# Two attention + feed-forward layers on one core: VectorE's exp in five passes instead of six, its steps and the side work paced by VectorE's queue, and the last 1024 queries of the first layer in chunks of 256

## The chip, the core and the metric

The kernel runs on one core of one Trainium2 chip. A core has five engines that run their own instruction streams and wait for one another through semaphores: TensorE (PE, matrix products; its weight loads are shown as PEld), VectorE (DVE), ScalarE (ACT, the engine with exp and tanh), GpSimd (POOL) and SyncE (SP, here the issuer of DMAs). The metric is the device time of one execution in microseconds (us); lower is better.

## The reference

Input x is 2048 tokens of 512 values, in bf16. The same weights are used twice:

```python
def _A_ref(x, wqkv, wo):                 # 32 heads of 16
    qkv = (x @ wqkv).reshape(B, S, 3, H, Dh).transpose(2, 0, 3, 1, 4)
    q, k, v = qkv[0], qkv[1], qkv[2]
    p = softmax(einsum("bhqd,bhkd->bhqk", q, k) * Dh ** -0.5)
    o = einsum("bhqk,bhkd->bhqd", p, v)
    return o.transpose(0, 2, 1, 3).reshape(B, S, D) @ wo

def _B_ref(x, w1, w2):                   # 512 -> 1792 -> 512
    return einsum("bsf,fd->bsd", silu(einsum("bsd,df->bsf", x, w1)), w2)

x = A_x
x = x + _A_ref(layernorm(x), A_wqkv, A_wo)
x = x + _B_ref(layernorm(x), B_w1, B_w2)
x = x + _A_ref(layernorm(x), A_wqkv, A_wo)
x = x + _B_ref(layernorm(x), B_w1, B_w2)
```

The exps are the bulk: 2 layers x 32 heads x 2048 x 2048 of them, against matrix products with an inner dimension of 16 for the scores.

## The kernel before

**Tiling.** Heads go in blocks of four (hb, eight of them), each head padded to 32 rows, so that four heads fill the 128 rows of PE. Queries go in chunks: three of 512 and two of 256 in both layers (CHUNKS, L163). A *block* is one chunk of one head block (class Block, L683). A *unit* is the scores of one head for 512 columns: 128 keys x 512 queries in a chunk of 512, two key tiles x 256 queries in a chunk of 256. Its scores are K (stationary) times Q (moving), into PSUM; then exp; then p (moving) times V with a column of ones (vaug, stationary), which accumulates both output and row sum in PSUM.

**Two streams of exp.** The function stream (L712) emits everything between the first and the last exp. Units are taken in *groups* of three and two in turn (new_group). A group's scores lie in one PSUM tile s_ps, and ACT makes p_sb of it in one instruction, 128x1536 or 128x1024 (L997). The tile p_sb of three units has two buffers, that of two units one (L213). Beside a group, one more unit can go to DVE (extra, chosen by spare, L749): its scores go into one of the three PSUM banks of the pool g, and exp_on_dve (L755) makes exp by bits: scale to an integer (PSUM to SBUF), split off mantissa and exponent by two bitwise instructions, two steps of a polynomial, and a last step that multiplies by the exponent and writes the bf16 tile pd_sb. These six instructions are a *chain*. spare gives a new unit only when the chain is empty, a count of DVE's outstanding work (V.behind) is below PITCH, and a bank is free. One step of the chain is emitted after each group; the product with V comes DEFER = 4 groups after the unit was taken, that is three after its last step.

**Side work.** Everything else is cut into *pieces* (class Piece) in four lanes: ends (a block's division by the row sum, finish), keys (keys of the next layer for the first six head blocks), main (output projection, layer norm, feed-forward of a finished chunk, then what the next layer needs of it) and side (queries of the next chunk, other keys, V). After each group, pieces are stepped while a credit lasts, at most 1024 columns of matmul; the credit grows by pace(g), the work to do in this phase over the groups left in it. Matmuls without use (keep_busy, fillers) are put in where the sum of PE's work over three groups is below BUSY. PE's instructions stay in the order in which they are emitted (pin, L192); DVE's and ACT's order follow from it.

**The layer boundary.** Layer 2 can't start before layer 1's last chunk has gone through its feed-forward. So the first six head blocks of layer 2's first chunk start *early*, on the first 1536 keys alone (EK, NE at L161; part "early"), and get the other 512 keys later (part "late"), with a factor that joins the two. The head blocks 6 and 7 ("full") need all keys. If a block's queries are not made when its scores are emitted, need (L817) steps pieces until they are, however many.

**Order of stages.** Layer 1: chunks 0, 1, 2 (512 queries), 3, 4 (256). Layer 2: early blocks, full and late blocks of chunk 0, chunks 1, 2, then 3 and 4 (256). Ahead of the first exp lie the loads, the layer norm of x and the first keys, V and queries; after the last exp the tail, that is projection, layer norm and feed-forward of the last 256 queries and the store. DVE's instructions are all issued by one helper, so their line is L36; the products on PE are L193, its transposes L197.

## Time and profile before

| what | us |
|---|---|
| median of 3 runs | 1985.38 (1978.69 to 1989.32) |
| the profiled execution, its own time | 1986.21 |
| its span, first to last instruction | 1984.4 |
| first exp of L997 starts at | 53.0 |
| last stage ends, tail begins | 1952.0 |
| ACT busy / exps of L997 alone | 1837.1 / 1773.4 |
| DVE busy / its exp passes (e_sb, pd_sb) | 1467.3 / 972.2 |
| PE busy | 1659.2 |
| mean granted clock of TensorE | 0.953 |

The exps are 765 of 128x1536 and 765 of 128x1024; the six DVE passes belong to 271 units. Busy time of ACT is a union: an exp starts while the one before it drains, so 1773.4 us is less than the sum of the durations. PE's busy time is modelled from the starts of pipelined matmuls and says little on how near PE is to its limit. The granted clock is that of TensorE alone; the profile shows it at half speed in some stretches, most of them in the second layer. The kernel's stages have different lengths, so the 40 equal slices of the page mix them; a table by stage is read in the prediction.

### The profile page before, as it was taken

The page shows a single profiled execution, that of the slowest core. Times are in us where ns is not written, and L with a number is a line of the kernel's source. Part 1 is how long each engine was busy: PE and PEld are TensorE (multiplying, and loading weights), DVE is VectorE, ACT ScalarE, POOL GpSimd, SP SyncE. Part 2 cuts the span into 40 slices and gives each one's busy share as a digit, 9 for nine tenths or more (in the row PEclk, how much of TensorE's full clock was granted, in tenths as well). Part 3 has the DMA queues.
Part 4 walks back from the last instruction along what each step waited for, and adds up shares of the span by engine and source line. Part 5 has one row for each costly group of instructions (what it writes and reads, how often), then busy time and mean ns, then how long its engine had stood idle before and what let it go on. Part 6 is the DMA issues. An engine that isn't in the chain of part 4 may idle for free.

```text
span 1984.4 us, 31764 instructions
## 1 busy us (share of the span) xinstructions
PE 1659.2 (84%) x12915; PEld 558.3 (28%) x12915; DVE 1467.3 (74%) x2966; ACT 1837.1 (93%) x1690; POOL 13.0 (1%) x17
## 2 busy tenths in 40 slices
PE   4888888888888888898888888888888788888887
PEld 2222222222222223333322222222222222233333
DVE  6798877777867787678866687776777777756764
ACT  5799999999999999999999798999999999889994
POOL 2000000000000000000000000000000000000000
PEclk9999999999999999999999889997999999879998
DMA  4000000000000000000000000000000000000000
GB/s 159 1 1 1 1 1 1 1 1 1 1 1 1 1 1 1 1 1 2 1 1 1 1 1 1 1 1 0 7 6 1 1 1 11 1 1 3 11 1 12
DMA packets 8403, 11.99 MB, mean 6 GB/s; under 512 B 320, under 2 KB 7232, under 8 KB 8256
## 3 DMA queue, kind: packets, MB, share of 16 engines
q1 hardware_dynamic: 8256, 9.96, 1.5%
q8 instruction: 101, 1.65, 0.3%
q14 instruction: 46, 0.38, 0.1%
HBM read 7.86 MB, written 2.10 MB: 5 GB/s over the span
## 4 chain that ended last, share of the span: by engine, by line
ACT 58%; PE 22%; DVE 15%; issue 5%; ACTq 0%; DVEq 0%
ACT p_sb L997 55%; PE g L193 14%; PE s_ps L193 7%; DVE e_sb L36 6%; ACT t_sb L601 2%; DVE qa L36 1%; DVE pd_sb L36 1%; DVE KT L36 1%; PE g L197 1%; DVE st L36 1%; DVE amaxp L36 1%; DVE oT L36 1%; DVE sel L36 1%; DVE x_sb L36 1%; ACT p_sb L1097 0%
## 5 line engine op out<-in xcount | busy, mean ns | idle before, releaser
L997 ACT ACTIVATE p_sb<-s_ps 128x1536 bf16<-128x1536 f32 (+1 forms) x1530 | 1773.4, 1283 | 94.2 <-PE g L193 67.7
L193 PE MATMUL s_ps<-QT,KT 32*128 32x512 bf16 (+1 forms) x4788 | 621.3, 348 | 231.7 <-ACT p_sb L997 213.1
L193 PE MATMUL g<-p_sb,vaug 128*32 128x512 bf16 (+1 forms) x4788 | 515.8, 355 | 1.8 <-ACT p_sb L997 0.6
L193 PEld LDWEIGHTS <-KT 32*128 32x128 bf16 x5120 | 229.9, 92 | 778.5 <-issue 749.7
L36 DVE SCALAR_TENSOR_TENSOR e_sb<-e_sb 128x512 f32<-128x512 f32 x542 | 370.4, 683 | 5.3
L36 DVE TENSOR_SCALAR e_sb<-g 128x512 int32<-128x512 f32 x271 | 186.6, 688 | 195.0 <-PE g L193 190.3
L36 DVE TENSOR_SCALAR e_sb<-e_sb 128x512 int32<-128x512 int32 x542 | 229.4, 423 | 13.6
L36 DVE SCALAR_TENSOR_TENSOR pd_sb<-e_sb 128x512 bf16<-128x512 f32 x271 | 185.8, 686 | 28.1 <-PE g L193 18.4
L193 PEld LDWEIGHTS <-vaug 128*32 128x32 bf16 x5120 | 145.4, 96 | 203.0 <-issue 187.3
L193 PE MATMUL g<-w_sb,hT 128*128 128x512 bf16 x448 | 139.4, 385 | 1.7 <-DVE KT L36 0.5
L36 DVE SCALAR_TENSOR_TENSOR hT<-t_sb,g 128x512 bf16<-128x512 f32 x105 | 72.0, 686 | 82.4 <-ACT t_sb L601 80.9
L193 PE MATMUL g<-xnT,w_sb 128*128 128x512 bf16 x336 | 116.7, 415 | 0.6 <-DVE xnT L36 0.5
L193 PE MATMUL g<-QT,KT 32*128 32x512 bf16 (+1 forms) x332 | 107.3, 353 | 2.8 <-DVE QT L36 0.8
L193 PE MATMUL g<-pd_sb,vaug 128*32 128x512 bf16 (+1 forms) x332 | 107.9, 355 | 0.0
L193 PE MATMUL g<-xnT,wq_pad 128*128 128x512 bf16 x280 | 95.6, 397 | 0.5 <-DVE QT L36 0.5
L193 PE MATMUL g<-xnT,wk_pad 128*128 128x512 bf16 x256 | 85.7, 404 | 5.6 <-DVE e_sb L36 1.6
L601 ACT ACTIVATE t_sb<-g 128x512 f32<-128x512 f32 x105 | 71.1, 677 | 1.7 <-PE g L193 1.7
L36 DVE CAST qa<-g 128x512 bf16<-128x512 f32 x70 | 48.0, 686 | 29.8 <-PE g L193 29.5
L36 DVE TENSOR_SCALAR QT<-g,shiftcol 128x512 bf16<-128x512 f32 x70 | 52.3, 747 | 19.1 <-PE g L193 18.2
L36 DVE CAST oT<-g 128x512 bf16<-128x512 f32 (+1 forms) x86 | 50.3, 585 | 19.3 <-PE g L193 18.8
L193 PEld LDWEIGHTS <-w_sb 128*128 128x128 bf16 x560 | 41.5, 100 | 80.0 <-issue 76.6
L36 DVE TENSOR_SCALAR KT<-g,onescol 128x512 bf16<-128x512 f32 x60 | 44.8, 747 | 16.4 <-PE g L193 16.2
(82 smaller groups left out, 810.5 us busy)
## 6 DMA issues: line engine op xcount, KB each, us to landing
w_sb<-in_B_w_dram SPq DMA_DIRECT2D x2, 1792.0 KB, 13.6
x_sb<-in_A_x_dram SPq DMA_DIRECT2D x4, 512.0 KB, 5.6
out_dram<-x_sb SPq DMA_DIRECT2D x8, 256.0 KB, 2.1
wqk_raw<-in_A_wqkv_dram SPq DMA_DIRECT2D x4, 256.0 KB, 7.2
wv_sb<-in_A_wqkv_dram SPq DMA_DIRECT2D x1, 512.0 KB, 8.5
wo_sb<-in_A_wo_dram SPq DMA_DIRECT2D x1, 512.0 KB, 8.7
```

Of the source, the lines that this page charges most:

```text
L36: return op(*args, **kw)
L193: ins = nc.tensor.matmul(*args, **kw)
L197: ins = nc.tensor.transpose(*args)
L601: nc.scalar.activation(t_sb[:, 0 : n * w], box["h"], ACT.Tanh, scale=0.5)
L997: nc.scalar.activation(p_sb[:, 0:n, :].rearrange("p a b -> p (a b)"), s_ps[:, 0:n, :].rearrange("p a b -> p (a b)"), ACT.Exp, bias=float(B ...
```

## The change

Four things are changed; the rest of the diff passes names through (L.chunks for CHUNKS, L.nch for NCH).

1. **exp_on_dve.** Five instructions instead of six: the exponent is no longer split off. M is the mantissa with a constant exponent (4 << 23), read as an integer; a cubic in M is made in two steps, and the last one adds it to the scaled integer. The result is an int32 whose upper half word is the bf16 of the exp; the product with V reads these halves at a step of two, so there is no tile pd_sb. The constants and the bias of ACT's exp change with it.

```diff
-            e = epool.tile([P, 3, 512], FP32, name="e_sb", tag="e")
+            bits = epool.tile([P, 512], I32, name="bits", tag="bits")
+            M = epool.tile([P, 512], I32, name="M", tag="M")
...
             def split():
                 V.tensor_scalar(
-                    out=w, in0=bits, scalar1=0x007FFFFF, scalar2=0x3F800000,
+                    out=M[:], in0=bits[:], scalar1=0x007FFFFF, scalar2=4 << 23,
                     op0=ALU.bitwise_and, op1=ALU.bitwise_or, share=0.5,
                 )
-                V.tensor_scalar(
-                    out=bits, in0=bits, scalar1=0x7F800000, scalar2=None, op0=ALU.bitwise_and,
-                    share=0.5,
-                )
...
+            def square():
+                box["u"] = epool.tile([P, 512], FP32, name="u", tag="u", bufs=2)
+                V.scalar_tensor_tensor(
+                    out=box["u"][:], in0=M[:], scalar=float(A1), in1=M[:], op0=ALU.add, op1=ALU.mult
+                )
+            def cube():
+                V.scalar_tensor_tensor(
+                    out=box["u"][:], in0=box["u"][:], scalar=float(A0), in1=M[:],
+                    op0=ALU.add, op1=ALU.mult,
+                )
             def last():
-                p = ppool.tile([P, 512], BF16, name="pd_sb", tag="pd", bufs=1)
+                u = box["u"][:].bitcast(I32)
                 V.scalar_tensor_tensor(
-                    out=p[:], in0=u, scalar=float(C0), in1=bits.bitcast(FP32),
-                    op0=ALU.add, op1=ALU.mult,
+                    out=u, in0=box["u"][:], scalar=float(CURVE), in1=bits[:],
+                    op0=ALU.mult, op1=ALU.add,
                 )
+                return u.bitcast(BF16).rearrange("p (n h) -> p n h", h=2)[:, :, 1]
```

2. **When the chain's steps and its product are emitted.** Instead of one step a group, steps are emitted while DVE's counted queue is under 1000 ns, with at most two units between their third step and their product. The product comes from two groups after the last step on, ahead of the products of the same block. spare may take the extra unit from the next block when the one at hand is nearly done; DEFER, now only a limit there, goes from 4 to 6.

```diff
-            if chain:
+            V.pass_time(1331 if n == GU else 905)
+            while chain and V.behind < 1000:
+                if len(chain) == 3 and n_begun - n_made >= 2:
+
+                    break
+                n_begun += len(chain) == 3
                 p = chain.pop(0)()
                 if not chain:
-                    later[chain_of[0] + DEFER] = [(p[:], extra[chain_of[0]])]
-            V.pass_time(1331 if n == GU else 905)
+                    late.append((g + 2, p, extra[chain_of[0]]))
```

```diff
-            todo += later.pop(g, [])
             todo += [(p_sb[:, i, :], u) for i, u in enumerate(grp)]
+            for x in [x for x in late if x[0] <= g]:
+
+                b = x[2][0]
+                at = next((i for i, (_, u) in enumerate(todo) if u[0] is b), None)
+                if at is not None:
+                    todo.insert(max(at, kept), x[1:])
+                    late.remove(x)
```

3. **Chunks by layer.** Layer 1 has two chunks of 512 and four of 256, layer 2 keeps three and two.

```diff
-    CHUNKS = [(512 * i, 512) for i in range(NKC - 1)] + [(S - 512, 256), (S - 256, 256)]
-    NCH = len(CHUNKS)
+    def query_chunks(n):
+
+        whole = [(512 * i, 512) for i in range(NKC - n)]
+        return whole + [(at, 256) for at in range(S - 512 * n, S, 256)]
...
-    L1 = make_layer(1, 0)
+    L1 = make_layer(1, 0, 2)
...
-    L1.nxt = L2 = make_layer(2, NE)
+    L1.nxt = L2 = make_layer(2, NE, 1)
```

4. **Pace and order of the side work.** pace counts what the feed-forward of the chunks of a phase will bring (chain_cost) instead of a constant 55000; layer 1's last chunk and layer 2's early blocks are one phase ("end") in which the early stage no longer asks for the largest credit; AHEAD goes from 28 to 20. After an even group up to 1536 columns of pieces are stepped, after an odd one 1024. main goes ahead of keys while the next two blocks have their queries, and a query piece is held back while eight QT tiles are in use (q_live). To make room in SBUF, the tail's tanh tile and the sums of the first three early blocks lie in tiles of attn.

```diff
+        def order():
+
+            near = all(b.QT in b.L.QT for b in waiting[:2])
+            return (ends, main, keys, side) if near else (ends, keys, main, side)
...
+        def chain_cost(L, c):
+
+            w = L.chunks[c][1]
+            per_tile = 6 * 512 + FT * 512 + (5 * 512 if L.nxt is not None else 0)
+            return w // P * per_tile + FT * CT * w
...
-            if ph[1] == -1:
-                return 3072
-            if ph[1] < NKC - 1:
-                todo += max(len(here) - 1, 0) * 2560
-            elif any(b.c == NCH - 2 for b in here):
-                todo += 55000
+            full = [b for b in here if b.part != "early"]
+            to_end = ph[1] == "end"
+            for L, c in {(b.L, b.c) for b in full}:
+                if to_end or c != max(b.c for b in full):
+                    todo += chain_cost(L, c)
...
-            while (credit[0] > 0 or hurry or sum(busy) < BUSY) and ran < 1024:
+            while (credit[0] > 0 or hurry or sum(busy) < BUSY) and ran < most:
...
-                    t_sb = epool.tile([P, 3 * 512], FP32, name="t_sb", tag="e")
+                    t_sb = achunk_pool.tile([P, 4, D], BF16, name="t_sb", tag="attn")
+                    t_sb = t_sb[:].rearrange("p a b -> p (a b)").bitcast(FP32)
```

## The prediction, made before the changed kernel was run

> **What bounds the kernel now.** I read the page first (engine totals, chain), then cut the span into its stages, then the groups by shape, the waits, and one timeline. The page says that ScalarE (ACT) carries the span:

> ```profile
> span 1984.4 us, 31764 instructions
> PE 1659.2 (84%) x12915; PEld 558.3 (28%) x12915; DVE 1467.3 (74%) x2966; ACT 1837.1 (93%) x1690; POOL 13.0 (1%) x17
> ACT 58%; PE 22%; DVE 15%; issue 5%; ACTq 0%; DVEq 0%
> ```

> To see where ACT's missing 7% lies I cut at the first exp of each stage, found by counting the exps of L997 in issue order. Columns: stretch, length, busy time (and count) of PE, PEld, DVE, ACT, POOL, then TensorE's granted clock.

> ```profile
> 287.00:514.10 227.10, 192.63 (x1298) 59.66 (x1298) 176.44 (x352) 223.81 (x205) 0.00 (x0) 0.98 0.00 1
> 740.80:859.70 118.90, 103.60 (x1209) 42.31 (x1209) 83.73 (x179) 117.53 (x112) 0.00 (x0) 1.00 0.01 1
> 978.90:1130.00 151.10, 129.59 (x867) 41.39 (x867) 102.51 (x228) 132.77 (x125) 0.00 (x0) 0.93 0.00 1
> 1130.00:1243.60 113.60, 95.37 (x619) 27.46 (x618) 84.98 (x171) 98.17 (x90) 0.00 (x0) 0.86 0.00 1
> 1708.30:1838.90 130.60, 114.41 (x1181) 43.58 (x1179) 80.70 (x171) 117.90 (x111) 0.00 (x0) 0.84 0.01 3
> 1952.00:1984.40 32.40, 20.73 (x115) 11.32 (x114) 14.02 (x34) 3.71 (x5) 0.00 (x0) 0.79 0.03 9
> ```

> The rows are layer 1's chunk 1 (512 wide) and chunk 3 (256 wide), layer 2's early blocks, the rest of its chunk 0, its chunk 3, and the tail. Length minus ACT busy is idle: 3.3, 1.4, 18.3, 15.4 and 12.7 us. Over all eleven stages (53.0 to 1952.0, 1899 us) it is 93 us. So ACT is the limit in the steady stages; idle time gathers at the layer boundary and where the clock fell. Two stages of one shape, 740.8 (clock 1.00, idle 1.4) and 1708.3 (0.84, 12.7), price the clock: 0.16 below full over 130.6 us cost 11.3 us.

> The boundary's largest single idle is seen in the timeline:

> ```profile
> 1120.56 0.74 DVE L36 TENSOR_SCALAR hT<-x_sb,mvb,lny 128x512 bf16<-128x512 bf16 x2
> ...
> 1122.32 1.87 PE L193 MATMUL g<-xnT,wk_pad 128*128 128x512 bf16 x4 [0.52 <-DVE xnT L36]
> ...
> 1127.26 0.75 DVE L36 TENSOR_SCALAR QT<-g,shiftcol 128x512 bf16<-128x512 f32 x1 [0.48 <-PE g L193]
> ...
> 1128.07 0.39 PE L193 MATMUL s_ps<-QT,KT 32*128 32x512 bf16 x3 [0.84 <-DVE QT L36]
> ```

> The next block's queries were not there, so layer norm, transposes, the last key piece and the query piece of head block 6 ran one after another with the scores queued behind them on PE. ACT stood still for 8.1 us, then 1.3 and 1.7 more at half clock.

> ```profile
> ACT p_sb L997 <- PE g L193: 67.7, 92, 3.5
> ACT p_sb L997 <- PE s_ps L193: 23.5, 28, 8.1
> ```

> The 8.1 is the longest of the second row. The first row, exps waiting for the product with V, is the usual wait: the 1024-wide p_sb has one buffer (L213), so its next exp needs the product's matmuls done.

> **The change, part by part.** *Units moved to DVE.* A unit is the exp of 128 keys x 512 queries of one head; two layers of 32 heads x 16 x 4 make 4096. In issue order DVE did 271 and now does 320; ACT keeps 3776 of 3825. The exps' 1773.4 us (page, first group) over 3825 units is 0.464 us a unit; 49 fewer make **-22.7 us**, all on ACT, which sets the end.

> ```profile
> L36 DVE SCALAR_TENSOR_TENSOR e_sb<-e_sb 128x512 f32<-128x512 f32 x542 | 370.4, 683 | 5.3
> L36 DVE TENSOR_SCALAR e_sb<-e_sb 128x512 int32<-128x512 int32 x542 | 229.4, 423 | 13.6
> L36 DVE TENSOR_SCALAR e_sb<-g 128x512 int32<-128x512 f32 x271 | 186.6, 688 | 195.0 <-PE g L193 190.3
> L36 DVE SCALAR_TENSOR_TENSOR pd_sb<-e_sb 128x512 bf16<-128x512 f32 x271 | 185.8, 686 | 28.1 <-PE g L193 18.4
> ```

> (The answer by shapes: mean ns, then idle before.) A unit was 0.688 + 2 x 0.423 + 2 x 0.683 + 0.686 = 3.586 us; now 0.688 + 0.423 + 3 x 0.683 = 3.160. DVE's exp goes from 271 x 3.586 = 972 to 320 x 3.160 = 1011 us, +39, beside ACT. In the stage at 287 us DVE was 176 of 227 us busy; 44 units for 36 add 139.0 - 129.1 = 9.9, so 186 of about 222, 84%: no bound by sum. The three passes now read int32 through the two-input form, which has no row here; bounds 423 (int32, one input) and 747 (QT's row), nearest 683, taken. At 747 DVE gains 61 us of work, 3% of the span, hidden by ACT.

> *The boundary.* The feed-forward of layer 1's chunks now runs earlier: as the early blocks begin, lane main holds pieces of 82,944 columns, before 117,760 (nearly two chunks of 256 instead of one, 40,000 each, and what follows them). In the new issue order the last transpose of its keys stands 26 exps ahead of block 6's first scores, and that block's queries are 15 exps ahead; before, both fell in one burst of eleven pieces. I take off the 8.1, 1.3 and 1.7 and add 1 for what is spread out: **-10**. Bounds: 0 (idle moves ahead) and -30 (both boundary stages fall to the 1.5% idle of the stage at 287: 33.7 - 0.015 x 265 = 29.7).

> *PE.* 512 more matmul pairs of 256 columns: the 256-wide stage at 740.8 idled 1.4 us, the 512-wide one 3.3 per twice the time, so 0. Pieces per pair of exps in the early stage rise from 1583 to 1730 columns, 14 matmuls of 512 in all; 41 fillers come too, issued where PE has room. One such matmul is 0.229 us:

> ```profile
> 39.78 2.75 PE L193 MATMUL g<-wv_sb,xnT 128*128 128x512 bf16 x12
> ```

> 14 x 0.229 = 3.2, and groups with three pieces instead of two come in bursts: **+3**, between 0 and +9 (fillers on the path too).

> *Reading every second half word.* PE reads DVE's probabilities as bf16 at a step of two. No row here has a moving operand with a step. Bounds: 0, and half rate, 320 x 0.229 = 73 us of PE. The half-clock stage says how much PE time reaches ACT: 0.16 x 130.6 = 20.9 us of PE lost, 11.3 us idle, 54%; so +39. I take **0**, as the pattern still advances one column per read.
> [...]

> *Pacing.* A unit's product with V now comes two exps after its last pass (three before), and passes go out only while DVE's queue counts under 1.0 us. So the last is done 1.0 + 0.69 = 1.7 us later against 2 exps, 1773.4 / 765 = 2.3 us: 0.6 us of margin. Behind it on PE are the two products that free the 1024-wide p_sb. **+2** for some late ones; bounds 0 and the third rival's 48. Layer norm and evictions of one more chunk are some 8 us of DVE (16 more each of oT 0.416, rec 0.198 and attn 0.284 for 8 fewer of 0.684, 0.247 and 0.415: 3.6; the rest small layer-norm steps at 0.16), hidden under ACT in the 256-wide stages, where DVE was 70% to 86% busy. The tail's tanh tile and three of the early sums move into tiles of attn; the instructions there keep the waits that they had, so 0. Head (53.0) and tail (32.4) stay. No DMA is added or moved; SP's and POOL's queues are as before.

> Sum: -22.7 - 10 + 3 + 2 = -27.7. The profiled execution took 1986.2 us (1.8 around its span), 0.8 above the median of the three runs; 1986.2 - 27.7 = **1958.5**.

> **Rivals.** *Idle moves* (0.15): the burst goes, but the early stage, at 1730 columns a pair, pays it back; 1986.2 - 22.7 + 5 = 1968. For: its idle was already 18.3 us; against: the chunk at 740.8 carries 1536 columns a pair and idles 1.4.
> *Half-rate reads* (0.08): 1958.5 + 39 = 1997. For: no row; against: the columns are no more than before.
> *Late DVE units* (0.13): the slower side. At the margin of 0.6 us, any wait of DVE on PE between the last passes decides; its waits ahead of e_sb<-g are 190.3 us over 158. Each such wait makes the unit 1.7 + 1.2 - 2.3 = 0.6 us late; if a quarter of that reaches ACT at every unit, 320 x 0.15 = 48: 2006. It beats the gain from 0.09 us per unit (27.7 / 320). Against: ahead of the 332 products from pd_sb the trace of before shows 0.0 us of idle, with DVE 83% busy in the first stage.

> **How the numbers follow.** The forecast has 0.64. I count 0.5%, 10 us, as what a measurement can tell: bounds 1975 and 1995. Faster: 0.62 of the forecast's, 0.12 of the first rival's, 0.02 of half-rate reads with a smaller share = 0.76. Slower: 0.11 late units, 0.04 half-rate = 0.15. Same: 0.09. Range: low 1932 (the boundary's -30 with neither PE's 3 nor pacing's 2 paid is 1986.2 - 22.7 - 30 = 1933.5); high 1990, into the case of late units, which leaves 0.08 of the 0.13 and some of the half-rate reads outside. That the clock alone can move a stage by 11 us is why the range is wide on both sides.

> **What would show it.** x755 of each exp shape; u passes near 683 ns; no 8 us wait of ACT on scores at the boundary, whose two stages should idle under 25 us together; matmuls g<-u,vaug as long as g<-p_sb,vaug (400 ns), with no idle waiting for DVE u. Waits of PE on u, or of exps on PE g well over 67.7 us, make it wrong, as would a lower granted clock.

## The result, and the profile after

| | median, us | range of 12 runs | profiled execution | its span |
|---|---|---|---|---|
| before | 1979.0 | 1971.2 to 1989.5 | 1986.2 | 1984.4 |
| after | 1995.6 | 1990.2 to 2004.0 | 1991.5 | 1989.7 |

(The kernel before was measured anew, beside the changed one on one chip.) The ratio of the times is 1.0083, 95% interval 1.0057 to 1.0109: the changed kernel is 0.8% slower, where 1958.5 us, 1.4% faster than the execution it was reckoned from, was forecast. The two profiled executions lie 7 us above and 4 us below their medians, so their traces differ by 5 us only; what was gained and what was lost can be read in them all the same. (The rest goes with TensorE's granted clock: the profiled execution of the changed kernel has the highest of its twelve, 0.950, the others down to 0.939; more on this in the last section.) The page of the changed kernel (span, busy time of the engines, the chain's shares by engine):

```profile
span 1989.7 us, 33776 instructions
PE 1601.6 (80%) x13838; PEld 585.6 (29%) x14036; DVE 1537.5 (77%) x2990; ACT 1818.5 (91%) x1671; POOL 13.0 (1%) x17
ACT 55%; PE 22%; DVE 15%; issue 7%; ACTq 0%; DVEq 0%
```

ACT has 18.6 us less to do, as it should, and its idle time has grown by more: 1989.7 - 1818.5 = 171.2 us against 147.3. (PE has 198 matmul records fewer than weight loads, so its busy time is not compared.) The answer by shapes shows the units and their cost, and which exps wait:

```profile
L1045 ACT ACTIVATE p_sb<-s_ps 128x1536 bf16<-128x1536 f32 x755 | 1123.0, 1487 | 20.7 <-PE s_ps L198 16.0 <-PE g L198 3.9
L1045 ACT ACTIVATE p_sb<-s_ps 128x1024 bf16<-128x1024 f32 x755 | 797.3, 1056 | 100.9 <-PE g L198 95.7 <-ACT t_sb L613 0.3
L36 DVE TENSOR_SCALAR bits<-g 128x512 int32<-128x512 f32 x320 | 220.7, 690 | 159.6 <-PE g L198 149.3
L36 DVE SCALAR_TENSOR_TENSOR u<-M 128x512 f32<-128x512 int32 x320 | 220.6, 689 | 13.9 <-PE g L198 5.3 <-PE g L202 0.5
L36 DVE SCALAR_TENSOR_TENSOR u<-u,bits 128x512 int32<-128x512 f32 x320 | 219.8, 687 | 6.6
L198 PE MATMUL g<-p_sb,vaug 128*32 128x512 bf16 x2358 | 306.1, 398 | 0.0
L198 PE MATMUL g<-u,vaug 128*32 128x512 bf16 x202 | 75.7, 407 | 7.9 <-DVE u L36 5.1 <-DVE oT L36 1.0 <-DVE bits L36 0.7
```

The five passes and the strided product cost what was assumed. The idle time is on the odd exps, 128x1024, and ends when PE has done a product (g). The waits say the same (sum, count, longest):

```profile
ACT p_sb L1045 <- PE g L198: 99.5, 134, 3.4
ACT p_sb L1045 <- PE s_ps L198: 16.0, 27, 3.8
```

Against the kernel before, 32 us more in 42 more waits on products; the 8.1 us wait on scores at the boundary is gone. By stage (columns as in the prediction's first table):

```profile
289.10:517.40 228.30, 185.67 (x1285) 59.22 (x1305) 188.06 (x353) 220.20 (x202) 0.00 (x0) 0.97 0.00 1
517.40:648.70 131.30, 104.80 (x1173) 42.70 (x1188) 92.45 (x184) 117.29 (x110) 0.00 (x0) 0.88 0.00 1
648.70:767.70 119.00, 99.28 (x1182) 44.33 (x1197) 92.04 (x198) 110.49 (x99) 0.00 (x0) 0.94 0.01 2
887.10:1015.30 128.20, 107.39 (x1212) 46.28 (x1226) 97.12 (x215) 114.12 (x104) 0.00 (x0) 0.89 0.01 1
1015.30:1153.50 138.20, 118.25 (x813) 37.15 (x825) 112.49 (x228) 128.35 (x117) 0.00 (x0) 0.98 0.00 1
1153.50:1262.40 108.90, 91.75 (x625) 27.52 (x634) 75.52 (x149) 100.22 (x93) 0.00 (x0) 0.97 0.00 1
```

These are layer 1's chunk 1, three of its four chunks of 256 (the *quarters*: 517.4, 648.7 and 887.1), and the two boundary stages. The boundary's idle is 9.9 + 8.7 = 18.5 us (33.7 before): a gain of 15. The quarters idle 14.0, 8.5 and 14.1 us (the fourth 5.3), where the chunk 2 of 512 and the two old chunks of 256 that they replace idled 3.4, 1.4 and 9.1. Chunk 1 has 8.1 for 3.3. All stages together: 118.8 against 93.1.

What such an idle spot looks like, in the timeline of the first quarter (start, length, engine, line, operation, shapes, count, and in brackets the idle time before and what ended it):

```profile
597.82 1.02 ACT L1045 ACTIVATE p_sb<-s_ps 128x1024 bf16<-128x1024 f32 x1
...
599.22 1.46 ACT L1045 ACTIVATE p_sb<-s_ps 128x1536 bf16<-128x1536 f32 x1
...
601.07 0.29 PE L198 MATMUL g<-p_sb,vaug 128*32 128x256 bf16 x2
601.18 2.36 ACT L1045 ACTIVATE p_sb<-s_ps 128x1536 bf16<-128x1536 f32 x2
...
603.59 0.29 PE L198 MATMUL s_ps<-QT,KT 32*128 32x256 bf16 x2 [2.12 <-ACT p_sb L1045]
...
603.93 0.39 PE L198 MATMUL g<-p_sb,vaug 128*32 128x256 bf16 x4
...
604.07 0.49 PE L198 MATMUL g<-p_sb,vaug 128*32 128x256 bf16 x6
...
604.70 1.02 ACT L1045 ACTIVATE p_sb<-s_ps 128x1024 bf16<-128x1024 f32 x1 [1.16 <-PE g L198]
```

The row at 601.18 joins two exps under the shape of the first: one of 1536, then one of 1024. So ACT ran 1024, 1536, **1536, 1024**, 1024: the exp at 601.18 was issued ahead of the odd one that was emitted before it. PE stood still for 2.12 us, since its next scores need the PSUM tile of the exp that came last; then the products and the next odd exp, which needs the one 1024-wide p_sb back, ran in series, and ACT idled 1.16 us. ACT's issue order, in which the kernel is built, shows it without any time:

```
L1045 Activation p_sb<-s_ps 128x1024
L613 Activation t_sb<-g 128x512
L1045 Activation p_sb<-s_ps 128x1536
L613 Activation t_sb<-g 128x512
L1045 Activation p_sb<-s_ps 128x1536
L1045 Activation p_sb<-s_ps 128x1024 x2
```

There are 17 such *turns* in the changed kernel, ten of them in the quarters, and 5 in the kernel before, three of them in the two boundary stages; the traces show the same counts. Each stands where one block gives way to the next, and where this line of the loop holds the products of the new block back (the same line in both kernels):

```python
if odd and kept <= GU and unit[0].out is None and min(Lane.banks + o_free) > g:
    break
```

It breaks when no bank of the pool g is free, by the loop's own book, for the new block's output. The book returns a bank later when DVE's counted queue is long (`late` in Lane.step). The products that would free the 1024-wide p_sb then come behind the next scores, the odd exp isn't ready in its turn, and the scheduler issues the even one first. I call this a *hold*. Counted in both traces alike, ACT idles 36.5 us before the five exps from each turn on in the changed kernel and 11.3 us in the kernel before; 22.3 of the 36.5 lie in the quarters. All its other idle time, from the first exp on, is 109.6 against 110.6 us, although the boundary gave 15 of it back. So the theory was: holds, by the exps out of turn that they cause; and a smaller loss somewhere that eats the boundary's gain.

### The profile page after: what moved, and what is told of

It reads as the page before. It is cut to its first block, busy times and chain, and to the rows that moved or that the text cites. A ratio compares the mean times of both kernels' runs of the same rounds, so it can differ in the third digit from the quotient of the medians.

```text
span 1989.7 us, 33776 instructions
## 1 busy us (share of the span) xinstructions
PE 1601.6 (80%) x13838; PEld 585.6 (29%) x14036; DVE 1537.5 (77%) x2990; ACT 1818.5 (91%) x1671; POOL 13.0 (1%) x17
## 4 chain that ended last, share of the span: by engine, by line
ACT 55%; PE 22%; DVE 15%; issue 7%; ACTq 0%; DVEq 0%
ACT p_sb L1045 51%; PE g L198 15%; PE s_ps L198 7%; DVE u L36 5%; ACT t_sb L613 3%; DVE bits L36 2%; DVE M L36 1%; DVE qa L36 1%; PE g L202 1%; DVE st L36 1%; DVE hT L36 1%; DVE QT L36 1%; DVE sel L36 1%; DVE oT L36 1%; DVE KT L36 1%
## 5 line engine op out<-in xcount | busy, mean ns | idle before, releaser
L1045 ACT ACTIVATE p_sb<-s_ps 128x1536 bf16<-128x1536 f32 (+1 forms) x1511 | 1749.6, 1271 | 121.5 <-PE g L198 99.5
L198 PE MATMUL s_ps<-QT,KT 32*128 32x256 bf16 (+1 forms) x5194 | 617.5, 333 | 288.9 <-ACT p_sb L1045 266.4
L198 PE MATMUL g<-p_sb,vaug 128*32 128x256 bf16 (+1 forms) x5194 | 498.1, 340 | 0.5 <-DVE hT L36 0.5
L36 DVE TENSOR_SCALAR bits<-g 128x512 int32<-128x512 f32 x320 | 220.7, 690 | 159.6 <-PE g L198 149.3
L36 DVE SCALAR_TENSOR_TENSOR u<-M 128x512 f32<-128x512 int32 x320 | 220.6, 689 | 13.9 <-PE g L198 5.3
L36 DVE SCALAR_TENSOR_TENSOR u<-u,M 128x512 f32<-128x512 f32 x320 | 220.0, 687 | 6.8
L36 DVE SCALAR_TENSOR_TENSOR u<-u,bits 128x512 int32<-128x512 f32 x320 | 219.8, 687 | 6.6
L36 DVE TENSOR_SCALAR M<-bits 128x512 int32<-128x512 int32 x320 | 135.7, 424 | 7.5
L36 DVE SCALAR_TENSOR_TENSOR hT<-t_sb,g 128x512 bf16<-128x512 f32 x105 | 72.1, 687 | 76.6 <-ACT t_sb L613 75.5
L198 PE MATMUL g<-QT,KT 32*128 32x256 bf16 (+1 forms) x438 | 128.5, 338 | 1.4 <-DVE QT L36 0.9
L198 PE MATMUL g<-u,vaug 128*32 128x256 bf16 (+1 forms) x438 | 117.0, 345 | 8.5 <-DVE u L36 5.3
L36 DVE CAST oT<-g 128x256 bf16<-128x256 f32 (+1 forms) x94 | 51.7, 550 | 44.6 <-PE g L198 44.2
L198 PEld LDWEIGHTS <-w_sb 128*128 128x128 bf16 x616 | 50.0, 102 | 75.8 <-issue 68.5
L36 DVE TENSOR_SCALAR QT<-g,shiftcol 128x512 bf16<-128x512 f32 x70 | 52.4, 749 | 19.1 <-PE g L198 17.6
L36 DVE CAST qa<-g 128x512 bf16<-128x512 f32 x70 | 48.1, 687 | 22.7 <-PE g L198 22.1
## 6 DMA issues: line engine op xcount, KB each, us to landing
w_sb<-in_B_w_dram SPq DMA_DIRECT2D x2, 1792.0 KB, 13.6
```

Source lines behind the costliest of these rows:

```text
L36: return op(*args, **kw)
L198: ins = nc.tensor.matmul(*args, **kw)
L1045: nc.scalar.activation(p_sb[:, 0:n, :].rearrange("p a b -> p (a b)"), s_ps[:, 0:n, :].rearrange("p a b -> p (a b)"), ACT.Exp, bias=float(B ...
```

## The experiments

Ratios are to the kernel before, measured beside each run, with the 95% interval. Holds and third rounds (explained in part 5) are counted in the order in which a kernel's instructions are emitted; the granted clock is the profiled execution's.

| run | us | ratio | units | holds | third rounds | clock |
|---|---|---|---|---|---|---|
| before | 1979.0 | 1 | 271 | 5 | 128 | 0.953 |
| after | 1995.6 | 1.0083 (1.0057 to 1.0109) | 320 | 17 | 15 | 0.950 |
| e1 after, order of all of ACT kept | 2265.5 | 1.1452 (1.1414 to 1.1490) | 320 | 17 | 15 | 0.834 |
| e2 before, the same | 2289.6 | 1.1574 (1.1532 to 1.1616) | 271 | 5 | 128 | 0.831 |
| e3 quarters undone | 1996.9 | 1.0095 (1.0061 to 1.0129) | 323 | 14 | 12 | 0.939 |
| e4 five passes alone | 1999.0 | 1.0099 (1.0064 to 1.0133) | 278 | 8 | 170 | 0.951 |
| e5 after, exps in turn | 1974.3 | 0.9991 (0.9970 to 1.0013) | 320 | 17 | 15 | 0.955 |
| e6 before, exps in turn | 1967.3 | 0.9955 (0.9935 to 0.9975) | 271 | 5 | 128 | 0.964 |
| e7 five passes, exps in turn | 1980.6 | 1.0025 (1.0008 to 1.0043) | 278 | 8 | 170 | 0.965 |
| e8 halves, exps in turn | 1969.3 | 0.9973 (0.9951 to 0.9995) | 323 | 14 | 12 | 0.957 |
| e9 after, no hold | 1967.7 | 0.9951 (0.9925 to 0.9978) | 320 | 0 | 11 | 0.955 |
| e10 before, no hold | 1964.2 | 0.9952 (0.9927 to 0.9976) | 271 | 0 | 128 | 0.965 |
| e11 five passes, no hold | 1974.6 | 0.9978 (0.9952 to 1.0005) | 278 | 0 | 169 | 0.966 |
| e12 the same, product earlier | 1951.3 | 0.9875 (0.9839 to 0.9912) | 287 | 0 | 0 | 0.967 |
| e13 after, no hold, one pass a group | 1944.0 | **0.9838** (0.9796 to 0.9879) | 314 | 0 | 6 | 0.970 |
| e14 the same with halves | 1963.4 | 0.9910 (0.9884 to 0.9937) | 315 | 0 | 5 | 0.952 |
| e15 halves, no hold | 1950.6 | 0.9852 (0.9824 to 0.9881) | 325 | 0 | 12 | 0.961 |
| e16 e9 with more fillers | 1970.1 | 0.9972 (0.9954 to 0.9989) | 320 | 0 | 12 | 0.957 |
| e17 e14 with AHEAD 28 | 1962.0 | 0.9936 (0.9913 to 0.9958) | 315 | 0 | 5 | 0.964 |
| e18 e13 with more fillers | 1962.5 | 0.9927 (0.9905 to 0.9948) | 308 | 0 | 2 | 0.977 |

**1. All of ACT in the order of emission (e1, e2).** A first try to stop the turns:

```diff
-            nc.scalar.activation(
+            ins = nc.scalar.activation(
                 p_sb[:, 0:n, :].rearrange("p a b -> p (a b)"),
...
             )
+            tc.keep_in_program_order(ins)
```

> The changed kernel with one thing added: ACT runs its exps in the order in which they are emitted. PE's order stays the same. In the changed kernel's trace an even (three-unit) exp stands ahead of the odd (two-unit) one that was emitted before it at 17 places, and the seven exps around each take 46 us in all over the undisturbed pitch of 2.25 us a pair; before the change there were 5 such places and 15 us. Theory swaps: most of that goes, 1955 to 1975 us, exps wait for products with V less than before the change (67.7 us), and fewer half-clock stretches than 36. Rival quarters (the 256-wide blocks and bursts of pieces load PE, and the places are only a sign of it): 1985 to 1997 us. Rival late units (products wait for DVE's passes): no change, 1990 to 1997.

> The kernel before with the same order kept on ACT; nothing else. Theory swaps: it loses 5 places worth 15 us, so about 1965 to 1973 us. Rivals: no change, 1975 to 1983.

Both kernels came out some 15% above the kernel before, far from every range given, and told nothing of the turns: the edit also binds each exp behind everything that was emitted before it on ACT. In the groups of e1:

```profile
L613 ACT ACTIVATE t_sb<-g 128x512 f32<-128x512 f32 x105 | 62.7, 597 | 247.2 <-PE g L198 247.2
```

Each of the 105 tanhs now holds the exps up until its matmuls are done, 2.4 us a piece. The edit was too wide. It did show what the freedom to issue a later exp ahead of a tanh is worth.

**2. Parts of the change (e3, e4).** The quarters undone (layer 1 again with two chunks of 256, the *halves* of the table), and the five passes put into the kernel before (with the tiles that the change moved for them):

```diff
-    L1 = make_layer(1, 0, 2)
+    L1 = make_layer(1, 0, 1)
```

> The changed kernel with layer 1's chunks as before (three of 512, two of 256); five passes, pacing and the rest as changed. In its issue order 14 even exps stand ahead of the odd one, for 17. Theory swaps: 3 places fewer, some 8 us: 1982 to 1992 us. Rival quarters: the 20 us that chunk 2 of layer 1 lost come back, 1970 to 1978. If the quarters bring the gain at the boundary that was forecast, that is lost again in both (10 us).

```diff
-            return [scale, split, step(wf, C2), step(u, C1), last]
+            return [scale, split, square, cube, last]
...
-                    later[chain_of[0] + DEFER] = [(p[:], extra[chain_of[0]])]
+                    later[chain_of[0] + DEFER] = [(p, extra[chain_of[0]])]
```

> The kernel before with the five passes alone, one step a group and chunks as before; the tail's tanh tile and three of the early sums moved as in the change, to make room. DVE does some 276 units for 271; 8 swapped places for 5. Theory swaps: -2 us for the units, +8 for the places: 1980 to 1990 us. Theory that half-word reads cost PE time: well above, 2000 and more. Theory that five passes themselves help: 1965 to 1975.

Neither run fell into a range given for it. The quarters alone are not the loss: without them the time is the same (1996.9 us, where the two theories gave 1982 to 1992 and 1970 to 1978). The five passes alone lose 20 us, with DVE 62 us *less* busy (1405.0 against 1467.3) and 7 more units. Their 1999.0 us lie above the range of the turns and just short of what slow half-word reads were to give, but the strided product takes 413 ns there against 399. What the two have in common with the changed kernel is more holds, 14 and 8 for 5, with 28.0 and 19.9 us of idle around them.

**3. The exps in their turn, and only they (e5 to e8).** An edge for the scheduler from each exp to the exp before it; tanhs and the rest may still move:

```diff
-        o_free = [0]
+        o_free, last_exp = [0], []
...
-            nc.scalar.activation(
+            with tc.issue_after(last_exp[0]) if last_exp else ExitStack():
+                ins = nc.scalar.activation(
...
+            last_exp[:] = [ins.ins]
```

> The changed kernel, with each exp of ACT bound to be issued behind the exp emitted before it, and nothing else bound (tanhs, square roots and copies may still go where they are ready). In the changed kernel 17 even exps (128x1536) are issued ahead of the odd one (128x1024) emitted before them, in the kernel before 5; the seven exps around each take 46 us more than their pitch elsewhere, against 15 us before. Theory A (these turns are the loss): no two 128x1536 exps in a row, the waits of the exps on PE's g fall from 99.5 us to below 75, and the time falls by 20 to 45 us, to 1950 to 1976 (ratio to before 0.985 to 0.998). Theory B (the turn follows from the products held back at a block's start, and ACT waits there in either order): the order changes, the waits on g stay at 90 to 105 us, and the time stays at 1988 to 2003 (ratio 1.005 to 1.012).

> The kernel before with the same bond between the exps. It has 5 such turns that cost 15 us together. Theory A: 1964 to 1975 us (ratio 0.992 to 0.998). Theory B: no change (ratio 0.998 to 1.002).

> The five passes alone (the kernel before otherwise, 1999.0 us, ratio 1.0099) with the bond between the exps. Its 8 such turns cost 24.8 us together, 10 us more than those of the kernel before. Theory A: 1974 to 1985 us (ratio 0.997 to 1.003), level with the kernel before. Theory B (the five passes themselves put other work at other places of PE, DVE and PSUM): 1992 to 2003 (ratio 1.006 to 1.012).

> The changed kernel with the quarters undone (1996.9 us, ratio 1.0095; 14 such turns that cost 36.5 us) and the bond between the exps. Theory A: 1960 to 1980 us (ratio 0.990 to 1.000); together with the changed kernel under the same bond it shows what the quarters are worth once the turns are gone. Theory B: 1990 to 2003 (ratio 1.006 to 1.012).

All four went the way of theory A, e5 by its time alone (its ratio, 0.9991, is a little above A's 0.998): by ratio, 0.9% off the changed kernel, 0.5% off the kernel before, 0.7% off the five passes, 1.2% off the halves. So the order itself costs, and more in the kernels with 14 and 17 turns than in the one with 5, though not in step with their number. But e5's waits did not fall below 75:

```profile
ACT p_sb L1046 <- PE g L198: 89.9, 134, 3.2
ACT p_sb L1046 <- PE s_ps L198: 8.8, 14, 3.8
```

The holds were still there, and ACT still idled 20.4 us around them (7.0 in e6): with the order right, the odd exp waits some 0.9 us for the held products (0.92 us at 827.63 and at 844.31 in e8). B was right in that part.

**4. No holds (e9, e10, e11).** The cause of the turns removed, the scheduler left free:

```diff
-                if odd and kept <= GU and unit[0].out is None and min(Lane.banks + o_free) > g:
+                if odd and kept <= GU and unit[0].out is None and min(Lane.banks + o_free) > g + 1:
```

> The changed kernel with one condition loosened: the products of a new block are held back only if no PSUM bank is due within one more group (g + 1 in place of g). That takes away the 17 holds at block turns of the changed kernel (5 in the kernel before), and with them the exps issued out of turn; the 1511 exps and the 320 units of DVE stay. In the changed kernel ACT idles 36.5 us in the stretches of five exps from these holds on, in the kernel before 11.3 us; with the exps bound to their turn, 20.4 us. Theory A (the holds are the loss, and the bank comes free in time): ACT's idle before exps falls by 20 to 35 us, and the time to 1960 to 1976 us (ratio 0.990 to 0.998). Theory B (DVE really is late with the bank, and PE only waits in another place): no better than with the exps bound, 1972 to 1980 (ratio 0.997 to 1.001), with PE waiting for DVE's oT or bits by 10 us and more.

> The kernel before with the same condition loosened: its 5 holds (11.3 us of idle around them) go. Theory A: 1963 to 1974 us (ratio 0.992 to 0.998). Theory B: as with the exps bound or worse, ratio 0.995 to 1.001.

> The five passes alone with the condition loosened: its 8 holds (19.9 us of idle around them) go. What is left against the kernel before without holds is the order of heads: of the runs of six products between two other kinds of matmul, 169 carry three products of one head (a third round on one group of 32 columns, some 220 ns by the starts in the traces, 234 against 443 to 461 ns from the first to the last), against 128 in the kernel before. Theory A (holds and third rounds are the whole of it): 41 rounds of 0.22 us, 9 us, above the kernel before without holds, ratio to before 0.998 to 1.003. Theory B (something else in the five passes costs): ratio above 1.005.

With one more group of patience in the book there is no hold and no exp out of turn, and PE hardly waits for the bank instead: in e9 its products wait 2.5 us for DVE's oT and 5.1 us for bits, its transposes 7.6 us for oT (6.3 in the changed kernel). The changed kernel falls from 1.0083 to 0.9951: 1.3%, 26 us, from this one constant, with the same 320 units. The waits of e9 and of e10:

```profile
ACT p_sb L1045 <- PE g L198: 84.2, 123, 3.0
ACT p_sb L1045 <- PE s_ps L198: 11.1, 18, 3.8
```

```profile
ACT p_sb L997 <- PE g L193: 54.4, 84, 3.5
ACT p_sb L997 <- PE s_ps L193: 20.1, 21, 8.0
```

The kernel before gains 0.5% by the same edit (theory A's range, where B's overlaps it), and e11 lies at the lower edge of A. So the holds explain why the change lost: with them out of both kernels, the two are level (0.9951 and 0.9952). They do not explain why, without them, the change only draws level, with exps on ACT that take 25 us less (1748.4 against 1773.4). Its exps wait 30 us longer on products.

The boundary's gain is not there either in these two runs. Its two stages (the early blocks, then the rest of chunk 0) in e9 and in e10:

```profile
993.20:1136.40 143.20, 125.85 (x834) 38.20 (x834) 114.82 (x230) 128.33 (x117) 0.00 (x0) 0.93 0.00 1
1136.40:1245.60 109.20, 93.00 (x628) 27.38 (x628) 76.00 (x151) 100.52 (x93) 0.00 (x0) 0.97 0.00 1
```

```profile
984.60:1129.00 144.40, 124.45 (x867) 40.44 (x867) 102.55 (x228) 132.24 (x125) 0.00 (x0) 0.96 0.00 1
1129.00:1233.60 104.60, 88.38 (x612) 26.25 (x609) 84.69 (x171) 97.54 (x89) 0.00 (x0) 0.94 0.00 1
```

ACT idles 23.6 us there in e9 and 19.2 in e10, although the long wait on scores (8.0 us) is still in e10 and is gone in e9. With the exps in turn it was the other way, 14.7 us in e5 and 23.9 in e6; each figure is of one execution. Over all stages e9 idles 97.1 us and e10 75.8. The 21 us between them have no single place: 4 in chunk 0, 5 in chunk 1, 5 in the quarters against what they replace, 4 at the boundary, 3 in the rest of layer 2.

**5. The third rounds (e11, e12).** The four heads of a block put their products on four groups of 32 columns of PE, and in the traces they run side by side: the starts of six products, of 400 ns each, lie within 234 ns, where twelve matmuls of 128 columns in a row took 0.229 us each (kernel before, at 39.78). Runs of six products between other matmuls show two lengths in the traces, from the first start to the last: 234 ns in the median, and 443 (kernel before) or 461 ns (e7). I put the long ones down to three products of one head, a third round; e12 tests it. Their number hangs on how many groups after its scores a DVE unit's product comes. In e12 it comes three after, not four:

```diff
-    DEFER = 4
+    DEFER = 3
```

> As the run before it, with the product of a DVE unit emitted three groups after its scores in place of four: no run of products has three of one head any more (0 against 169), 287 units against 278, 1524 exps against 1527. Theory A (third rounds bound PE where ACT waits for it): up to 169 x 0.22 = 37 us less on PE, of which a third to two thirds shows, and 4 us less on ACT: 14 to 28 us below the run before it, ratio to before 0.985 to 0.995. Theory B (PE has room for them): only the 4 us of ACT, ratio 0.996 to 1.002. Should u come late for the earlier product, PE waits for DVE's u over 10 us, and the time is above that.

Theory A again, 23 us below e11, of which the 9 units more explain 4. The products' row in e11 and in e12:

```profile
L193 PE MATMUL g<-p_sb,vaug 128*32 128x512 bf16 (+1 forms) x4781 | 519.5, 350 | 4.3 <-DVE hT L36 1.8 <-DVE oT L36 1.6 <-ACT p_sb L1005 0.9
```

```profile
L193 PE MATMUL g<-p_sb,vaug 128*32 128x512 bf16 (+1 forms) x4770 | 479.5, 350 | 2.2 <-DVE bits L36 0.9 <-DVE hT L36 0.8 <-ACT p_sb L1005 0.4
```

As many matmuls, each as long, 40 us less of PE's time: 169 x 0.22 = 37 were expected. Half of it reached the end. In the traces, 116 of 217 runs of six 512-wide products are long ones in e11, and 10 of 224 in e12.

Of the 20 us that the five passes alone lost, some 14 come with the holds (by ratio, e4 to e11 is 0.0121, before to e10 0.0048). The rest, e11 above e10, is 5 us by ratio and 10 by the medians, and the two intervals overlap. The 41 third rounds more, 9 us of PE, may be one reason for it. The boundary may be another, which no expectation named: its one long wait, 8.0 us in e10, takes 13.1 in e11 (13.2 in e4, 15.0 in e12), now put down to a product.

```profile
ACT p_sb L1005 <- PE g L193: 67.4, 80, 13.1
```

How the two share the rest is not shown. No run points to the speed of DVE.

**6. What is left (e13 to e18).** The changed kernel has only 15 third rounds for 128, so its level draw in e9 hides a second gain that went somewhere. e13 undoes the pacing by the queue, e15 the quarters, e14 both, all without holds:

```diff
-            while chain and V.behind < 1000:
-                if len(chain) == 3 and n_begun - n_made >= 2:
-
-                    break
-                n_begun += len(chain) == 3
+            if chain:
                 p = chain.pop(0)()
```

> The changed kernel without holds, with the pacing by DVE's queue undone: one pass of a DVE unit per group, its product two groups after the last pass as now. 314 units (320), 1513 exps (1511), 6 third rounds (11). Theory P (the pacing by the queue is where the rest went: passes of two units crowd DVE and its evictions come late): ratio to before 0.982 to 0.990, against 0.9951 with it. Theory Q (the quarters are where it went): 0.993 to 0.997 here, and the gain comes with the halves instead. Theory R (more units mean a fuller PE per exp, whatever paces them): 0.993 to 0.998 in this run and in the next two.

> As the run before it, with the quarters undone too: 315 units, 1513 exps, 5 third rounds. Theory P: 0.979 to 0.988, some 5 us below the run before it (the worth of the quarters with the exps bound to their turn). Theory Q: 0.984 to 0.990. Theory R: 0.990 to 0.996. Below 0.9875 it would be the fastest kernel here.

> The changed kernel without holds, with the quarters undone and the pacing by the queue kept: 325 units, 1509 exps, 12 third rounds. Theory P: 0.991 to 0.995 (the quarters' 0.2 per cent). Theory Q: 0.984 to 0.990. Theory R: 0.991 to 0.996.

No theory holds in all three. Either edit alone brings 1%, as if it were the cause (P in e13, Q in e15); both together bring 0.4% (R in e14). The worth of the quarters changes its sign with the pacing: with the queue they cost 1% (e9 against e15), with one pass a group they gain 0.7% (e13 against e14). e13 has the lowest ratio of the study, 1.6% below the kernel before, with an interval that overlaps those of e12 and e15. The row of its exps with their waits, and that of e10:

```profile
L1045 ACT ACTIVATE p_sb<-s_ps 128x1536 bf16<-128x1536 f32 (+1 forms) x1513 | 1747.6, 1290 | 75.5 <-PE g L198 62.2 <-PE s_ps L198 8.5 <-ACT p_sb L1045 0.3
```

```profile
L997 ACT ACTIVATE p_sb<-s_ps 128x1536 bf16<-128x1536 f32 x1530 | 1773.4, 1287 | 77.2 <-PE g L193 54.4 <-PE s_ps L193 20.1 <-ACT p_sb L997 0.8
```

Here the units' gain arrives whole: against the profiled execution of e10, 25.8 us less in exps, 1.7 less in idle before them, and a span 26.7 us shorter. (This execution is the fastest of e13's six; by ratio e13 lies 1.1% below e10, some 23 us.)

The idle time of ACT goes along with the half-clock time of PE over the runs without holds up to here (by the granted clock, 117 us in e13, 179 in e9, 189 in e14, with 75.5, 99.8 and 100.2 us of idle before the exps), so e16 and e18 fill PE's pauses with matmuls that nothing needs, and e17 changes three groups of side work to see how far the time moves by a trifle:

```diff
-    FULL, BUSY = 216.0, 1330.0
+    FULL, BUSY = 216.0, 1550.0
```

> The changed kernel without holds, with the level up to which PE's pauses are filled raised from 1330 to 1550: 276 filler matmuls in place of 138, and the same 320 units, 1511 exps, no hold and 12 third rounds (11). Theory C (half-clock stretches follow pauses of PE and cost ACT's time): half clock falls from 179 us to below 130, ACT's idle by 15 us and more, and the time from 1967.7 to 1940 to 1958 (ratio 0.980 to 0.990). Theory D (the fillers' 138 x 0.23 = 32 us only load PE): half clock stays, ratio 0.996 to 1.006.

> The halves with one pass a group and no holds (0.9910) with AHEAD 28 in place of 20: other work beside the exps changes in three groups at the end of layer 1 only. If the differences of 0.5 per cent between kernels without holds are chance of the schedule, this run may lie anywhere from 0.984 to 0.996; if they have causes, it lies at 0.989 to 0.993.

> The fastest kernel so far (quarters, one pass a group, no holds, 0.9838) with the fill level at 1550: 318 fillers (124), 308 units (314), 2 third rounds (6). Theory C: half clock from 117 us to below 90, but 2.8 us more on ACT: ratio 0.978 to 0.986. Theory D: ratio 0.988 to 1.000.

Theory C falls as a remedy. In e16 138 more fillers left the time alone, but they hardly moved the clock either (half clock 171 us for 179), so the link itself was not put to the test there. In e18 the clock rose to 0.977, the highest of all, half clock fell to 92 us, and the time rose 0.9%, into D's range; 2.8 us of that go with its 6 units fewer. What the fillers themselves cost, and where, was not tried. e17 (0.9936) came out just above the narrower of its two bands and within the wider, and its interval overlaps e14's, so it doesn't tell chance of the schedule from a cause. What stays open is about 1%: why the changed kernel without holds needs either the halves or the even pace to show its gain.

## Why the prediction was wrong

- **Units moved, -22.7: right.** 320 units, x755 of each shape, exps' busy time down by 23.8. It was ACT's work, and it went.
- **DVE's passes, +39 beside ACT: right.** The two-input passes on int32 take 689 and 687 ns (683 was taken); a unit 3.18 us (3.16). DVE is busy 77% of the span.
- **The boundary, -10: right for these two traces, not shown apart from the holds.** The 8.1 us wait is gone and the two stages idle 15 us less. But three of the five turns of the kernel before stood in these stages, and apart from turns and holds the runs disagree: with the exps in turn the change saves 9 us there (14.7 in e5, 23.9 in e6), without holds nothing (23.6 in e9, 19.2 in e10).
- **Strided reads, 0: right.** 407 against 398 ns. The 0 was my estimate: the kernel before has no product that reads at a step.
- **PE, +3: its 0 for the quarters failed in this kernel.** It was read from the old stage at 740.8, which idled 1.4 us. The quarters idle 28 us more than the stages that they replace, and ten of the 17 turns stand there with 22 us of idle. By themselves they have no fixed price: undone, they change nothing while the holds stand (e3), 4 to 5 us with the exps in turn (e5 against e8, intervals that overlap), and without holds they cost 1% or gain 0.7%, by the pacing. The change also took away 113 of the 128 third rounds, a gain for PE that no term had.
- **Pacing, +2 (bounds 0 and 48): the step that failed.** It was costed as units that come late for their product. They hardly do: PE waits 5.3 us for u. The sum left out that the change moves the loop's book of PSUM banks, and through it the place of the products and the order of the exps; it kept the waits of the exps on products as they were. That cost 25 us of idle at the holds (36.5 for 11.3), and taking the holds out gave back 26 us (e9). The 8 holds of the five passes alone, the 14 with the quarters undone and the 17 of the whole change say that no single part makes them all; no run takes the pacing alone out while the holds stand, so its share is argued and not shown. The sign that the prediction named against itself, waits on PE's g well over 67.7 us, came true: 99.5. So did the lower clock: 0.939 to 0.950 over the twelve executions, where 29 of the kernel before, run beside e9, had 0.947 to 0.967.

The slip behind it is plain. I took from the issue order *how many* exps and units there are, and where two pieces stand at the boundary; I did not read the exps as a sequence. Two of 128x1536 in a row, 17 times for 5, stood in it before any run. Of the rivals, the half-rate reads fell (407 ns); that their 1997 us is nearly the measured time is chance. The late units had the right sign for the wrong reason. The moved idle is not seen in the changed kernel (early stage 9.9 us of idle for 18.3) nor with the exps in turn (7.1 in e5, 13.3 in e6), but it may be there without holds (14.9 in e9, 12.2 in e10). The result lies 6 us above the range.

The account of the two spans: ACT's work -18.6; its idle +25 at the holds, -15 at the boundary, -2 in head and tail, and some 16 more in the other stages (a hold within a boundary stage is in two of these): together +5.3. The 16 are not explained; they belong to what e9, e13 and e15 left open.

## What to carry to other kernels

Where a scheduler orders an engine's instructions, compare the *sequence* of the bounding engine's instructions before and after, not their counts; the 17 pairs out of turn here, with 36.5 us of idle around them, can be seen without a run. A loop that keeps a book of buffers and holds work back by it can lose more than the wait that it avoids: test the hold with one step more of patience. When a product is moved by a group, count which array group each lands on: here six products took 234 ns from the first start to the last, and 443 to 461 ns where, by the reading of part 5, three shared a group.

## What the runs showed of the hardware

Turns and half clock go together: 15 of the 17 turns are followed within 7 us by the start of such a stretch, where only 12% of all moments are (in the kernel before 4 of 5, against 9%). So a turn may cost more than the idle of ACT beside it; how much is not shown, since e9, without a turn, still has 179 us of half clock, for 199.

Between executions of one kernel, which issue the same instructions, the time followed the clock. The twelve of the changed kernel run from 2004.0 us at 0.939 to 1990.2 at 0.949, the twelve of e10 from 1973.2 at 0.958 to 1956.2 at 0.971. Straight lines through them give 12.4 and 11.4 us for 0.01 of clock, that is about 60% of the 20 us of PE's time that 0.01 stands for, near the 54% that the prediction took from two stages. Which of the two is the cause is open: a wait of ACT also makes a pause on PE.

Raising the clock with fillers did not buy time: 0.970 to 0.977 with 0.9% more time (e13, e18), and at the same 0.970 an execution of e18 took 1966.3 us and one of e13 1938.8.
